# Three hinted widths in the experts' conditional first layer, and side work in smaller, evenly spaced steps

## The chip, the cores and the metric

One core of one Trainium2 chip. The metric is device time in microseconds of one execution. The kernel before takes 965.94 us (median of 3 runs, 965.71 to 967.29).

## The reference

Attention with a window of 128 keys over 4 sequences of 576 tokens, then a mixture of 8 experts with the two best of each token, then a gated feed-forward block:

```
attn = softmax(q k^T / 8 + bias, masked) v           # 2304 tokens x 512
noisy = x w_gate + log1p(exp(x w_noise)) * noise      # 2304 x 8
top2  = the two largest of each row, weights by softmax
for e in range(8):                                    # w1: 512 x 1024, w2: 1024 x 512
    out[rows of e] += weight * (relu(x[rows] @ w1[e]) @ w2[e])
xn  = out / rms(out) * rms_g
y   = (silu(xn @ w_gate2) * (xn @ w_val)) @ w_out     # 512 -> 1536 -> 512
```

How many rows an expert gets is known only when the routing has run. With the inputs of the case, experts 1 to 7 get 571, 575, 544, 545, 556, 606 and 584 rows.

## The kernel before, in words

The program is one hand-ordered stream. After attention and routing, experts 0 to 7 follow one another, then the gated block runs in products over quads of token tiles. Each expert has room for 640 rows (CAP). Every product is made of three float16 products of high and low halves (hi*hi, lo*hi, hi*lo), so each value leaves PSUM twice: ACT writes the high half, DVE the low one.

An expert e of 1 to 7 has five stages on TensorE (PE):

- **first layer**, rows 0 to 383: 8 column blocks of 12 matmuls of 384 columns (`first_steps`, L199). After each block ACT writes hh (L204) and DVE hl (L205). PSUM has three buffers for the even blocks and two for the odd ones.
- **second layer**, three blocks of 128 rows, 24 matmuls of 512 columns each (`second_steps`, L259). Each block ends with an ACT copy ys (L316) and a store to ybuf on SP's queue (L322).
- **tail**: the first layer for rows 384 to 639 (`tail_steps`, L234), 96 matmuls. Its width depends on the row count: the table `WIDTHS` has 160, 192, 224 and 256 columns, and the program holds one copy of the 96 matmuls for each. A register of PE, `arm`, counts how many of the first three widths are too small, and two nested conditions (`by_arm`, L215) pick the copy. The widest copy stands first in the program, the narrowest last; a copy that isn't the last ends with a branch over the rest. Then ACT and DVE take the four pairs of blocks out of PSUM (hh L244, hl L245).
- a **fourth block** of the second layer (again L259), which needs the four hl in turn.
- the **halves** block (`halves_steps`, L275) for rows 512 to 639, whose second half runs in full only where arm is over 1 (L281).

`drive` interleaves side work with these stages. Each side is a generator with a due column and a pace: when the columns that PE has been given pass the due column, the side's next step is emitted, and the due column grows by the pace. An expert is some 112,000 such columns long (first layer to 36,864, second layer to 73,728, tail to 92,160, fourth block to 104,448). The sides are:

- `weight_steps`: 8 loads of 512 KB for expert e+1, in 16 steps of one ACT conversion (L136) and one DVE subtraction (L138), from 2,000 at 3,000. The first three loads are issued at the end of the expert ahead (`ahead`, at 106,000).
- `m2_steps`: six 512 KB pieces of the gated block's float64 weights per expert, from 46,000 at 3,100. A piece takes three steps: (1) load of a later piece, and ACT's conversion hi of the piece before (L767), (2) DVE's lo of the piece before (L770), ACT's square sq (L779) and three DVE operations u (L780 to L782), (3) DVE's r (L785).
- `weight_sums`: sums of weights for the later products, a chunk of six steps on DVE (L817), ACT (L820) and GpSimd (L823). Experts 3, 4, 5 and 6 make one chunk each, from 30,000 at 5,500, and expert 7 makes three at 3,000 (`SUM0`).
- `row_steps`: transposing loads of the token rows xA and xB (L183).

All loads and stores of these stages stand in one queue, SP's, in program order. The weight loads and the m2 loads share four staging buffers `st`.

Of the kernel before, what the change touches and what calls it, by code (L numbers as in the profile page):

```python
# [31 lines left out]
WIDTHS = (160, 192, 224, 256)  # L32
# [3 lines left out]
SOON, SUM0, SUMS = 3, 3000, 4400  # L36
# [8 lines left out]
def attention_moe_swiglu(  # L45
# [52 lines left out]
    arm = consts.tile([P, E], I32, name="arm")  # L98
# [110 lines left out]
    def by_arm(value, ways, lo=0):  # L209

        if len(ways) == 1:
            ways[0]()
            return
        half = len(ways) // 2
        with tc.If(value > lo + half - 1) as cmp:  # L215
            by_arm(value, ways[half:], lo + half)
        with cmp.Else():
            by_arm(value, ways[:half], lo)

    def tail_steps(w1h, w1l, xT, cs, arm):  # L220

        hh = hpool.tile([P, FC, GW], F16, name="hh")
        hl = hpool.tile([P, FC, GW], F16, name="hl")
        yield hh, hl
        w = cs.stop - cs.start
        hps = [ps.tile([P, 2, w], F32, name=f"mm{i % 2}", bufs=MM[i % 2]) for i in range(FC // 2)]

        def columns(most):
            for f in range(FC):
                n = 0  # L230
                for w1, xo in ((w1h, 0), (w1l, 0), (w1h, KC)):
                    for c in range(KC):
                        now = most if n else w
                        nc.tensor.matmul(hps[f // 2][:, f % 2, :now], w1[:, c, f * P:(f + 1) * P],  # L234
                                         xT(xo + c, slice(cs.start, cs.start + now)),
                                         start=(n == 0), stop=(n == 3 * KC - 1))
                        n += 1

        by_arm(arm, [functools.partial(columns, x) for x in WIDTHS])
        mean = 3 * KC * WIDTHS[1]  # L240
        for i, hp in enumerate(hps):
            yield mean
            fs = slice(2 * i, 2 * i + 2)
            nc.scalar.activation(hh[:, fs, :w], hp, AF.Relu)  # L244
            nc.vector.scalar_tensor_tensor(hl[:, fs, :w], hp, 0.0, hh[:, fs, :w], op0=OP.max, op1=OP.subtract)  # L245
            yield mean
# [18 lines left out]
    def halves_steps(yp, hh, hl, w2h, w2l, i, arm):  # L265
# [15 lines left out]
        with tc.If(arm > 1) as cmp:  # L281
            rows(1, 3 * FC)
# [11 lines left out]
    def expert_steps(e, *pieces):  # L294
# [6 lines left out]
        if pieces == (LAST,) and e:  # L301
            steps = tail_steps(w1h, w1l, x, *pieces, arms[e])
# [4 lines left out]
        for cs in pieces:  # L307
            for c in range(cs.start, cs.stop, P):
                yp = ps.tile([P, DM], F32, name="acc", bufs=2)
                halved = e and c + P == CAP  # L310
                if halved:
                    yield from halves_steps(yp, hh, hl, w2h, w2l, (c - pieces[0].start) // P, arms[e])
# [15 lines left out]
    with ExitStack() as actx:  # L328
# [403 lines left out]
        wide = work.tile([P, E], F32, name="wide", bufs=1)  # L732
        nc.vector.tensor_scalar(wide, tot, float(GW + WIDTHS[0]), None, op0=OP.is_gt)
        for i, w in enumerate(WIDTHS[1:-1]):
            nc.vector.scalar_tensor_tensor(arm if i == len(WIDTHS) - 3 else wide, tot, float(GW + w), wide,
                                           op0=OP.is_gt, op1=OP.add)
# [20 lines left out]
    def m2_steps(parts):  # L757

        sts, last = [], None
        for i in range(len(parts) + 3):  # L760
# [3 lines left out]

            if last:
                r, sc, hi, lo = last
                nc.scalar.activation(hi, r, AF.Copy, scale=sc)  # L767
            yield
            if last:
                nc.vector.scalar_tensor_tensor(lo, r, sc, hi, op0=OP.mult, op1=OP.subtract)  # L770
            if not 2 <= i < len(parts) + 2:
                continue
            _, sc, hi, lo = parts[i - 2]

            wl, wh = (sts[i - 2].rearrange("p (n two) -> p n two", two=2)[:, :, j] for j in range(2))
            sq = dec.tile([P, DM], F32, name="sq")
            u = dec.tile([P, DM], I32, name="u")
            r = dec.tile([P, DM], F32, name="r")
            nc.scalar.activation(sq, wh.bitcast(F32), AF.Square)  # L779
            nc.vector.tensor_scalar(u, wh, 3, 0x3FFFFFFF, op0=OP.logical_shift_left, op1=OP.bitwise_and)  # L780
            nc.vector.scalar_tensor_tensor(u, wl, 29, u, op0=OP.logical_shift_right, op1=OP.bitwise_or)  # L781
            nc.vector.scalar_tensor_tensor(u, wh, -0x40000000, u, op0=OP.bitwise_and, op1=OP.bitwise_or)  # L782
            yield

            nc.vector.scalar_tensor_tensor(r, sq, 1.265625 * 2.0 ** -30, u.bitcast(F32), op0=OP.is_ge, op1=OP.mult)  # L785
# [64 lines left out]
    EARLIER = {3: [(0, 0)], 4: [(1, 0)], 5: [(0, 1)], 6: [(1, 1)]}  # L850
    BESIDE = len(EARLIER)
# [3 lines left out]

    def read_arms():
        _, values = nc.values_load_multi_w_load_instructions(arm[0:1, 0:E], engines=[EngineType.PE])
        arms.update(enumerate(values))
        yield

    def ahead(e):
        if e < E:
# [6 lines left out]
          (40000, 4000, mix()), (60000, 4000, read_arms()), (70000, 5000, ahead(2)))  # L869
    for e in range(1, E - 1):  # L870
        drive(itertools.chain(*(expert_steps(e, cs) for cs in HALVES)),
              (2000, 3000, coming.pop(e + 1)), (106000, 5000, ahead(e + 2)),
              (1000, 2000, row_steps(e, HALVES[1])), (46000, 2000, row_steps(e + 1, HALVES[0])),
              (30000, 5500, weight_sums([spool], sw, EARLIER.get(e, ()))),
              (46000, 3100, m2_steps([m2_part(i) for i in range(6 * (e - 1), 6 * e)])))
# [308 lines left out]
    with ExitStack() as c:  # L1184
        mp, xpool = block_pools(c, "tile")
        xq = xpool.tile([P, 28, QW], F16, name="xq")
        for at in chunks[BESIDE:BESIDE + SOON]:
            sw[at] = [xpool.tile([P, 2, 2, 2, P], F16, name=f"sw{at[0]}{at[1]}_{j}") for j in range(2)]
        drive(itertools.chain(*(expert_steps(E - 1, cs) for cs in HALVES)), (1000, 2000, row_steps(E - 1, HALVES[1])),
              (0, SUM0, weight_sums([spool, mp], sw, chunks[BESIDE:BESIDE + SOON])),  # L1190
# [100 lines left out]
```

## Time and profile before

The profiled execution took 972.34 us by the same clock as the runs, and its span from the first to the last instruction is 970.6 us.

| | |
|---|---|
| median of 3 runs | 965.94 us |
| profiled execution: time, span | 972.34 us, 970.6 us |
| PE busy | 930.8 us (96%) |
| DVE busy | 647.5 us (67%) |
| ACT busy | 453.9 us (47%) |
| GpSimd busy | 214.5 us (22%) |
| mean granted TensorE clock | 0.991 |

Busy time is the union of an engine's instructions. A matmul's end is modelled, so consecutive matmuls overlap in the record, and a gap shorter than this overlap isn't shown as idle. [...] "issue" is idle time in which an engine waited for nothing that the profile shows. PE's sequencer, which reads the instructions and runs ahead of the matrix unit, has rows of its own, named PEldq.

### The profile page before, as it was taken

Reading aid. Unit: us, or ns where it says so; the run is one execution under the profiler, and the core shown is the slowest. Engines: PE = TensorE matmul, PEld = TensorE weight load, DVE = VectorE, ACT = ScalarE, POOL = GpSimd, SP = SyncE. Lnnn points to the kernel's source line nnn. Section 1 sums busy time; section 2 is a strip of 40 time slices with the busy share of each in tenths; the row PEclk is TensorE's granted clock in tenths of the full one; section 3 lists DMA queues with packets and bytes.
Section 4 is the critical chain, followed back from the end, with each engine's and each line's share of the span. In section 5 each row is a group of like instructions: output and inputs, shape, how many; then the busy total and the mean of one; then the engine's idle time right before and its main releaser. Section 6 shows DMA issues by size and latency. Waiting matters only on the chain.

```text
span 970.6 us, 19059 instructions
## 1 busy us (share of the span) xinstructions
PE 930.8 (96%) x7478; PEld 661.0 (68%) x7478; DVE 647.5 (67%) x1482; ACT 453.9 (47%) x911; POOL 214.5 (22%) x255
## 2 busy tenths in 40 slices
PE   7998999999989989999999899999999999999997
PEld 5997888656656555556565586687488558848864
DVE  6799975536677878777777267798169618925840
ACT  7997873444354544454634245335224413532320
POOL 5566763000000101010103235610501131030000
PEclk9999999999999999999999999999999999999999
DMA  7988674767584849393931332510511250032000
GB/s 222 314 238 235 188 183 151 196 189 219 145 270 126 265 130 276 103 271 112 270 118 37 96 87 46 130 34 1 138 37 33 42 133 22 12 76 46 1 13 35
DMA packets 146691, 127.19 MB, mean 131 GB/s; under 512 B 98320, under 2 KB 117264, under 8 KB 146576
## 3 DMA queue, kind: packets, MB, share of 16 engines
q1 hardware_dynamic: 140816, 106.73, 40.5%
q0 software_dynamic: 5760, 18.88, 6.1%
q8 instruction: 78, 1.28, 0.6%
q14 instruction: 37, 0.30, 0.1%
HBM read 76.55 MB, written 26.74 MB: 106 GB/s over the span
## 4 chain that ended last, share of the span: by engine, by line
PE 61%; DVE 19%; DMA 6%; ACT 4%; issue 4%; SPq 2%; POOL 2%; another core or an unknown queue 0%; DVEq 0%; POOLq 0%; ACTq 0%
PE mm L1113 22%; PE acc L1085 11%; PE mm L199 7%; PE acc L259 7%; PE acc L454 4%; DMA st<-in_moe_w 3%; DVE w2l L138 2%; PE mm L440 2%; DVE sums L817 2%; PE mm L234 2%; PE mm L412 2%; PE acc L275 2%; DVE u L781 2%; DVE hl L205 1%; DVE u L782 1%
## 5 line engine op out<-in xcount | busy, mean ns | idle before, releaser
L259 PE MATMUL acc<-w2h,hh 128*128 128x512 f16 x264 | 101.7, 385 | 7.2 <-issue 4.7
L259 PE MATMUL acc<-w2h,hl 128*128 128x512 f16 x264 | 101.9, 386 | 4.3 <-DVE hl L245 3.5
L259 PE MATMUL acc<-w2l,hh 128*128 128x512 f16 x264 | 101.5, 385 | 0.0
L823 POOL TENSOR_TENSOR sw<-sums,sw 128x256 f16<-128x256 f32 x28 | 26.2, 945 | 335.7 <-ACT sw L820 335.6
L259 PEld LDWEIGHTS <-hh 128*128 128x128 f16 x528 | 51.7, 99 | 68.2 <-issue 8.1
L199 PE MATMUL mm<-xA,w1h 128*128 128x384 f16 (+2 forms) x576 | 97.3, 308 | 0.8 <-issue 0.8
L1085 PE MATMUL acc<-oh__3309,pgh 128*128 128x512 f16 (+2 forms) x228 | 83.3, 368 | 0.1
L1085 PE MATMUL acc<-ol__3310,pgh 128*128 128x512 f16 (+2 forms) x228 | 83.3, 368 | 0.0
L1085 PE MATMUL acc<-oh__3309,pgl 128*128 128x512 f16 (+2 forms) x228 | 83.2, 368 | 0.0
L199 PEld LDWEIGHTS <-w1h 128*128 128x128 f16 x640 | 59.7, 98 | 33.7 <-issue 2.3
L1113 PE MATMUL mm<-xq,sw 128*128 128x256 f16 x672 | 78.1, 273 | 3.0 <-DMA xq<-xg 3.0
L205 DVE SCALAR_TENSOR_TENSOR hl<-mm,hh 128x384 f16<-128x384 f32 (+2 forms) x80 | 39.7, 500 | 60.3 <-ACT hh L204 60.3
L1085 PEld LDWEIGHTS <-pgh 128*128 128x128 f16 x456 | 44.1, 98 | 49.2 <-ACT pgh L1065 0.6
L1113 PEld LDWEIGHTS <-sw 128*128 128x128 f16 x672 | 65.6, 98 | 11.5 <-issue 3.5
L454 PE MATMUL acc<-v,pf 128*128 128x96 f32 x544 | 72.1, 275 | 0.0
L432 ACT ACTIVATE pr<-ss,nm 128x256 f32<-128x256 f32 (+1 forms) x144 | 63.1, 488 | 10.4 <-DVE nm L423 8.6
L454 PEld LDWEIGHTS acc<-v,pf 128*128 128x128 f32 x544 | 67.9, 195 | 0.1
L423 DVE CUSTOM_DVE_ANT_0 ss<-mm,bias 128x256 f32<-128x256 f32 (+1 forms) x144 | 54.0, 397 | 13.7 <-PE mm L412 6.6
L1122 DVE TENSOR_TENSOR gt<-mm,p 128x512 f32<-128x512 f32 x24 | 16.6, 691 | 66.1 <-PE mm L1113 62.6
L1134 ACT ACTIVATE p<-mm 128x256 f32<-128x256 f32 x48 | 18.3, 382 | 77.5 <-PE mm L1113 75.5
L199 PE MATMUL mm<-xA,w1l 128*128 128x384 f16 (+2 forms) x288 | 53.8, 308 | 0.0
L259 PEld LDWEIGHTS <-hl 128*128 128x128 f16 x264 | 26.1, 99 | 40.6 <-DVE hl L245 7.7
(215 smaller groups left out, 2076.5 us busy)
## 6 DMA issues: line engine op xcount, KB each, us to landing
st<-in_moe_w SPq DMA_DIRECT2D x64, 512.0 KB, 4.4
raw<-in_qkv SPq DMA_DIRECT2D x17, 512.0 KB, 5.5
ybuf<-ys SPq DMA_DIRECT2D x33, 256.0 KB, 2.5
st<-in_moe_w_gate SPq DMA_DIRECT2D x12, 512.0 KB
st<-in_moe_w_val SPq DMA_DIRECT2D x12, 512.0 KB, 4.3
st<-in_moe_w_out SPq DMA_DIRECT2D x12, 512.0 KB, 4.4
v<-in_qkv SPq DMA_DIRECT2D x18, 279.0 KB, 7.3
out<-ys SPq DMA_DIRECT2D x17, 256.0 KB, 2.0
```

The lines of the kernel that those rows point to most:

```text
L138: nc.vector.scalar_tensor_tensor(*last, op0=OP.mult, op1=OP.subtract)
L199: nc.tensor.matmul(hp[:, :w], w1[:, c, f * P:(f + 1) * P], xT(xo + c, cs), start=(n == 0), stop=(n == 3 * KC - 1))
L205: nc.vector.scalar_tensor_tensor(hl[:, f, hs], hp[:, :w], 0.0, hh[:, f, hs], op0=OP.max, op1=OP.subtract)
L234: nc.tensor.matmul(hps[f // 2][:, f % 2, :now], w1[:, c, f * P:(f + 1) * P], xT(xo + c, slice(cs.start, cs.start + now)), start=(n == 0), ...
L259: nc.tensor.matmul(yp, hx[:, f, i * P:(i + 1) * P], w2[:, f, :], start=(n == 0), stop=(n == 3 * FC - 1))
L275: nc.tensor.matmul(yp[d * P // 2:(d + 1) * P // 2, j * DM // 2:(j + 1) * DM // 2], hx[:, f, at:at + P // 2], w2[:, f, d * DM // 2:(d + 1) ...
L423: nc.vector.tensor_tensor_reduce(out=d["ss"][:, j, c0:], in0=d["sp"][:, j, c0:], in1=bias[kind][:, heads(d["hp"])[j], c0:], scale=-1.0 / K ...
L432: nc.scalar.activation(d["pr"][:, j, c0:], d["ss"][:, j, c0:], AF.Exp, scale=-1.0, bias=d["nm"][:, j:j + 1])
L454: nc.tensor.matmul(xps[t, hp // 2][:, h % 4, :VN], ph[:, j, kk, :], v32[t - 1 + kk][:, h * DV:h * DV + VN], start=(kk == k0), stop=(kk == 1))
L823: nc.gpsimd.tensor_tensor(out=here[k][1], in0=x, in1=here[k][0], op=OP.subtract)
L1085: nc.tensor.matmul(op[:, ds], px[:, f, cs], w[:, f, ds], start=(k == 0), stop=(k == 3 * GC - 1))
L1113: nc.tensor.matmul(pp, w(a, pa, c), xq[:, 4 * b + 2 * pb + c, :], start=(n == 0), stop=(n == 5))
```

## The change

Four things are edited.

1. `WIDTHS` loses 160. Two flags per expert (more than 192 rows in the tail, more than 224) replace the count in `arm`. The tail has three copies. The outer condition takes the narrow copy, last in the program, in its Else part; the halves condition reads the first flag.
2. The flags are no longer read all at once during expert 0. `read_arms(e)` reads two of them ahead of the third second-layer block of expert e, and puts a branch hint there, whose value is the first flag.
3. `m2_steps` is cut differently: ACT's hi and sq and two of the u operations in step one, the third u and the lo of the piece before in step two, r in step three. It starts at 30,000 and runs at 3,800.
4. The weight steps run at 2,500 in place of 3,000. Experts 4 and 6 make one chunk of sums each, from 41,000 at 8,000, and expert 7 makes five at 2,500.

```
-WIDTHS = (160, 192, 224, 256)
+WIDTHS = (192, 224, 256)
-SOON, SUM0, SUMS = 3, 3000, 4400
+SOON, SUM0, SUMS = 3, 2500, 4400
-    arm = consts.tile([P, E], I32, name="arm")
+    arm = consts.tile([P, E, 2], I32, name="arm")
...
+    def read_arms(e):
+        _, arms[e] = nc.values_load_multi_w_load_instructions(arm[0:1, e], engines=[EngineType.PE])
+        tc.mark_branch_hint_location(f"tail{e}", hint=arms[e][0], engines=[EngineType.PE])
+
+    def by_arm(e, ways):
+
+        wide, full = arms[e]
+        with tc.If(wide, label=f"tail{e}") as cmp:
+            with tc.If(full) as cmp2:
+                ways[2]()
+            with cmp2.Else():
+                ways[1]()
+        with cmp.Else():
             ways[0]()
...
-        mean = 3 * KC * WIDTHS[1]
+        mean = 3 * KC * WIDTHS[0]
...
-        with tc.If(arm > 1) as cmp:
+        with tc.If(arms[e][0]) as cmp:
...
+                if e and c + P == GW:
+                    read_arms(e)
...
+            here = 2 <= i < len(parts) + 2
             if last:
                 r, sc, hi, lo = last
                 nc.scalar.activation(hi, r, AF.Copy, scale=sc)
-            yield
+            if here:
+                wl, wh = (sts[i - 2].rearrange("p (n two) -> p n two", two=2)[:, :, j] for j in range(2))
+                sq = dec.tile([P, DM], F32, name="sq")
+                u = dec.tile([P, DM], I32, name="u")
+                nc.scalar.activation(sq, wh.bitcast(F32), AF.Square)
+                nc.vector.tensor_scalar(u, wh, 3, 0x3FFFFFFF, op0=OP.logical_shift_left, op1=OP.bitwise_and)
+                nc.vector.scalar_tensor_tensor(u, wl, 29, u, op0=OP.logical_shift_right, op1=OP.bitwise_or)
+            yield
+            if here:
+                nc.vector.scalar_tensor_tensor(u, wh, -0x40000000, u, op0=OP.bitwise_and, op1=OP.bitwise_or)
             if last:
                 nc.vector.scalar_tensor_tensor(lo, r, sc, hi, op0=OP.mult, op1=OP.subtract)
...
-    EARLIER = {3: [(0, 0)], 4: [(1, 0)], 5: [(0, 1)], 6: [(1, 1)]}
-    BESIDE = len(EARLIER)
+    EARLIER = {4: [(0, 0)], 6: [(1, 0)]}
+    BESIDE = 4
...
-          (40000, 4000, mix()), (60000, 4000, read_arms()), (70000, 5000, ahead(2)))
+          (40000, 4000, mix()), (70000, 5000, ahead(2)))
...
-              (2000, 3000, coming.pop(e + 1)), (106000, 5000, ahead(e + 2)),
+              (2000, 2500, coming.pop(e + 1)), (106000, 5000, ahead(e + 2)),
...
-              (30000, 5500, weight_sums([spool], sw, EARLIER.get(e, ()))),
-              (46000, 3100, m2_steps([m2_part(i) for i in range(6 * (e - 1), 6 * e)])))
+              (41000, 8000, weight_sums([spool], sw, EARLIER.get(e, ()))),
+              (30000, 3800, m2_steps([m2_part(i) for i in range(6 * (e - 1), 6 * e)])))
...
-              (0, SUM0, weight_sums([spool, mp], sw, chunks[BESIDE:BESIDE + SOON])),
+              (0, SUM0, weight_sums([spool, mp], sw, [(0, 1), (1, 1), *chunks[BESIDE:BESIDE + SOON]])),
```

Three places show how the order moves. The first is PE ahead of expert 1's tail. Before (line numbers of the kernel before):

```order
L259 LDWEIGHTS hl
L259 MATMUL acc<-w2h,hl 128x512
L215 COMPARE_AND_BRANCH x2
L234 LDWEIGHTS w1h
L234 MATMUL mm_4007<-xB,w1h 128x256
```

And in the change (its own line numbers; L263 is the second layer, L238 the tail):

```order
L263 MATMUL acc<-w2h,hl 128x512
L210 TENSOR_LOAD arm
L1287 BRANCH_PREFETCH_HINT
L263 LDWEIGHTS hh
L263 MATMUL acc<-w2h,hh 128x512
...
L263 MATMUL acc<-w2h,hl 128x512
L216 COMPARE_AND_BRANCH
L217 COMPARE_AND_BRANCH
L238 LDWEIGHTS w1h
L238 MATMUL mm_4011<-xB,w1h 128x256
```

The read and the hint stand 48 PE instructions (24 matmuls of 512 columns) ahead of the first branch, and two copies of 192 instructions lie between that branch and the narrow copy.

The second is DVE around the tail of expert 3 (hl is the low half taken out of PSUM; u, r and the low half vl are the m2 step). Before:

```order
L782 SCALAR_TENSOR_TENSOR u<-st,u 128x512
L245 SCALAR_TENSOR_TENSOR hl<-mm_5764,hh 128x2x256
L785 SCALAR_TENSOR_TENSOR r<-sq,u 128x512
L245 SCALAR_TENSOR_TENSOR hl<-mm_5765,hh 128x2x256
L770 SCALAR_TENSOR_TENSOR vl__3308<-r,gain,vh__3307 128x512
L780 TENSOR_SCALAR u<-st 128x512
L781 SCALAR_TENSOR_TENSOR u<-st,u 128x512
L782 SCALAR_TENSOR_TENSOR u<-st,u 128x512
L245 SCALAR_TENSOR_TENSOR hl<-mm_5766,hh 128x2x256
L785 SCALAR_TENSOR_TENSOR r<-sq,u 128x512
L245 SCALAR_TENSOR_TENSOR hl<-mm_5767,hh 128x2x256
```

In the change (L249 is hl, L777, L778 and L781 are u, L783 is lo, L790 is r):

```order
L249 SCALAR_TENSOR_TENSOR hl<-mm_5569,hh 128x2x256
L790 SCALAR_TENSOR_TENSOR r<-sq,u 128x512
L249 SCALAR_TENSOR_TENSOR hl<-mm_5570,hh 128x2x256
L777 TENSOR_SCALAR u<-st 128x512
L778 SCALAR_TENSOR_TENSOR u<-st,u 128x512
L249 SCALAR_TENSOR_TENSOR hl<-mm_5571,hh 128x2x256
L781 SCALAR_TENSOR_TENSOR u<-st,u 128x512
L783 SCALAR_TENSOR_TENSOR vl__3306<-r,gain,vh__3305 128x512
L249 SCALAR_TENSOR_TENSOR hl<-mm_5572,hh 128x2x256
```

Between two hl there are now at most two m2 operations, where there were up to four, and lo no longer stands right behind the r on which it depends through ACT.

The third is SP's queue from the end of expert 1 into expert 2. Before:

```order
L322 DMA ybuf<-ys 128x512
L116 DMA st<-in_moe_w 128x4x256 x2
L320 DMA ybuf<-ys 64x2x256 x2
L116 DMA st<-in_moe_w 128x4x256
L183 DMA_TRANSPOSE xB<-xrows 128x8x128 x2
L116 DMA st<-in_moe_w 128x4x256
L116 DMA st<-in_moe_w 128x2x512 x4
L183 DMA_TRANSPOSE xA<-xrows 128x8x128
L763 DMA st<-in_moe_w_gate 128x1024
```

In the change (L326 is the store of the halves block, L766 the m2 load):

```order
L326 DMA ybuf<-ys 64x2x256 x2
L116 DMA st<-in_moe_w 128x4x256
L183 DMA_TRANSPOSE xB<-xrows 128x8x128
L116 DMA st<-in_moe_w 128x4x256
L183 DMA_TRANSPOSE xB<-xrows 128x8x128
L116 DMA st<-in_moe_w 128x2x512 x4
L766 DMA st<-in_moe_w_gate 128x1024 x3
L183 DMA_TRANSPOSE xA<-xrows 128x8x128 x2
```

The fourth weight load has moved ahead of the second xB transpose, and three m2 loads ahead of the xA transposes.

## Rows read from the trace of the kernel before

**Rows 1.** PE's waits, 200 to 640 us: us in total, times, longest.

```profile
PE acc L259 <- issue: 4.7, 2, 2.6
PE mm L234 <- issue: 4.4, 4, 2.2
PE acc L259 <- DVE hl L245: 3.5, 3, 1.6
PE acc L259 <- ACT hh L244: 2.5, 4, 0.8
```

**Rows 2.** Windows: experts 1 to 7, cut at each one's first matmul.

```profile
core 0: us, PE busy (x) PEld busy (x) DVE busy (x) ACT busy (x) POOL busy (x), PEclk, DMA share, GB/s
204.58:252.01 47.43, 47.43 (x340) 29.32 (x338) 31.93 (x53) 23.51 (x44) 0.00 (x0) 1.00 0.61 173
252.01:302.21 50.20, 47.77 (x340) 29.16 (x339) 35.00 (x59) 24.31 (x47) 0.00 (x0) 1.00 0.67 200
302.21:353.09 50.88, 47.28 (x340) 27.71 (x339) 39.06 (x66) 24.64 (x49) 4.29 (x4) 1.00 0.69 198
353.09:405.88 52.79, 49.81 (x340) 29.53 (x339) 40.79 (x69) 26.64 (x52) 4.29 (x4) 0.97 0.64 191
405.88:456.18 50.30, 48.10 (x341) 29.08 (x339) 38.15 (x64) 23.81 (x48) 4.29 (x4) 1.00 0.72 200
456.18:511.18 55.00, 52.95 (x386) 33.41 (x385) 43.04 (x73) 26.40 (x52) 4.30 (x4) 0.97 0.63 188
511.18:566.47 55.29, 52.65 (x387) 33.34 (x385) 26.01 (x58) 17.72 (x38) 14.88 (x18) 0.97 0.29 73
```

**Rows 3.** Windows inside experts 4, 6 and 7 with a lowered clock; columns as above.

```profile
400.30:403.60 3.30, 3.30 (x18) 1.40 (x18) 3.13 (x6) 0.12 (x1) 0.00 (x0) 0.50 0.00 0
499.30:502.60 3.30, 3.30 (x9) 1.22 (x8) 2.12 (x5) 1.67 (x3) 0.00 (x0) 0.50 0.02 5
553.90:557.20 3.30, 2.76 (x7) 1.04 (x8) 1.73 (x4) 2.38 (x4) 0.00 (x0) 0.50 0.35 107
```

**Rows 4.** Line L215 near the tails of experts 1, 2 and 6: ns min/median/max.

```profile
L215 PEldq COMPARE_BRANCH  x2: 82/1886/3690, 231.9 to 235.6; - x2
L215 PEldq COMPARE_BRANCH  x2: 82/3011/5940, 279.7 to 285.8; - x2
L215 PEldq COMPARE_BRANCH  x3: 70/208/3867, 483.5 to 494.9; - x3
```

**Rows 5.** Line L857, the read of all eight arms in expert 0.

```profile
L857 PEldq TENSOR_LOAD <-arm x1: 777/777/777, 190.3 to 190.3; - x1
```

**Rows 6.** Timeline of PE: first tail and next second-layer matmul, experts 1 and 3.

```profile
235.75 0.53 PE L234 MATMUL mm<-xB,w1h 128*128 128x256 f16 x4
...
243.88 0.38 PE L259 MATMUL acc<-w2h,hh 128*128 128x512 f16 x1
...
334.34 0.49 PE L234 MATMUL mm<-xB,w1h 128*128 128x256 f16 x4 [0.81 <-issue]
...
341.31 0.38 PE L259 MATMUL acc<-w2h,hh 128*128 128x512 f16 x1
```

**Rows 7.** Timeline of DVE, ACT and PE, third and fourth pair of expert 3's tail.

```profile
343.52 0.74 DVE L770 SCALAR_TENSOR_TENSOR vl__3308<-r,gain,vh__3307 128x512 f16<-128x512 f32 x1
344.18 0.42 DVE L780 TENSOR_SCALAR u<-st 128x512 int32<-128x512 int32 x1
...
345.97 0.68 DVE L245 SCALAR_TENSOR_TENSOR hl<-mm,hh 128x512 f16<-128x512 f32 x1
346.57 0.68 DVE L785 SCALAR_TENSOR_TENSOR r<-sq,u 128x512 f32<-128x512 f32 x1
...
347.28 0.72 ACT L767 ACTIVATE vh__3307<-r,gain 128x512 f16<-128x512 f32 x1 [3.36 <-DVE r L785]
...
346.71 0.39 PE L259 MATMUL acc<-w2h,hl 128*128 128x512 f16 x1 [1.58 <-DVE hl L245]
```

**Rows 8.** ACT's waits, 200 to 560 us: us in total, times, longest.

```profile
ACT w1h L136 <- DMA st<-in_moe_w: 28.3, 15, 4.0
```

More of the change, by code (lines that the diff above doesn't have):

```diff
@@ L207, in first_steps, with tail_steps @@
             yield 6 * w
-    def by_arm(value, ways, lo=0):
-        if len(ways) == 1:
-            ways[0]()
[L213 to L220, printed above, removed]
+    def read_arms(e):
[9 more added lines that the diff above has]
+        with cmp.Else():
+            ways[0]()
+    def tail_steps(w1h, w1l, xT, cs, e):
         hh = hpool.tile([P, FC, GW], F16, name="hh")
@@ L237, in columns @@
                         n += 1
-        by_arm(arm, [functools.partial(columns, x) for x in WIDTHS])
-        mean = 3 * KC * WIDTHS[1]
+        by_arm(e, [functools.partial(columns, x) for x in WIDTHS])
+        mean = 3 * KC * WIDTHS[0]
         for i, hp in enumerate(hps):
@@ L263, in second_steps, with halves_steps @@
                 yield 6 * DM
-    def halves_steps(yp, hh, hl, w2h, w2l, i, arm):
+    def halves_steps(yp, hh, hl, w2h, w2l, i, e):
         def rows(j, most):
@@ L301, in expert_steps @@
         if pieces == (LAST,) and e:
-            steps = tail_steps(w1h, w1l, x, *pieces, arms[e])
+            steps = tail_steps(w1h, w1l, x, *pieces, e)
         else:
@@ L310, in expert_steps @@
                 halved = e and c + P == CAP
+                if e and c + P == GW:
+                    read_arms(e)
                 if halved:
-                    yield from halves_steps(yp, hh, hl, w2h, w2l, (c - pieces[0].start) // P, arms[e])
+                    yield from halves_steps(yp, hh, hl, w2h, w2l, (c - pieces[0].start) // P, e)
                 else:
@@ L731, in attention_moe_swiglu @@
         nc.vector.scalar_tensor_tensor(over, most, float(CAP), few[:, :1], op0=OP.is_gt, op1=OP.max)
[L732 to L736, printed above, removed]
+        for i, w in enumerate(WIDTHS[:-1]):
+            nc.vector.tensor_scalar(arm[:, :, i], tot, float(GW + w), None, op0=OP.is_gt)
     m2w = ctx.enter_context(tc.tile_pool(name="m2w", bufs=1, side="right", reuse_waits="tile"))
@@ L767, in m2_steps @@
                 nc.scalar.activation(hi, r, AF.Copy, scale=sc)
+            if here:
[5 more added lines that the diff above has]
+                nc.vector.scalar_tensor_tensor(u, wl, 29, u, op0=OP.logical_shift_right, op1=OP.bitwise_or)
             yield
+            if here:
+                nc.vector.scalar_tensor_tensor(u, wh, -0x40000000, u, op0=OP.bitwise_and, op1=OP.bitwise_or)
             if last:
                 nc.vector.scalar_tensor_tensor(lo, r, sc, hi, op0=OP.mult, op1=OP.subtract)
-            if not 2 <= i < len(parts) + 2:
+            if not here:
                 continue
+            yield
             _, sc, hi, lo = parts[i - 2]
-            wl, wh = (sts[i - 2].rearrange("p (n two) -> p n two", two=2)[:, :, j] for j in range(2))
-            sq = dec.tile([P, DM], F32, name="sq")
-            u = dec.tile([P, DM], I32, name="u")
             r = dec.tile([P, DM], F32, name="r")
[L779 to L782, printed above, removed]
-            yield
             nc.vector.scalar_tensor_tensor(r, sq, 1.265625 * 2.0 ** -30, u.bitcast(F32), op0=OP.is_ge, op1=OP.mult)
```

4 lines of the change are left out of this document (removed).

## The prediction

> **What bounds the kernel now.** I read PE's waits first. PE is busy for 96% of the span, so the kernel is bound by TensorE, and only its idle time and its clock can give anything back. In the stretch of the experts [rows 1] the waits are of two kinds. 9.1 us (4.7 and 4.4) are "issue", at the first matmul behind a branch: PE waited for no engine and no load. 6.0 us (3.5 and 2.5) are the fourth block of the second layer waiting for hl and hh of the tail, which DVE and ACT write.
>
> Then I cut the trace at the first matmul of each expert [rows 2]. Expert 1 takes 47.43 us and is busy throughout: that is the price of an expert at a tail of 192 columns. The others are measured against it.
>
> - Experts 2, 4 and 5 have the same work and take 50.20, 52.79 and 50.30 us: 2.8, 5.4 and 2.9 us too many.
> - Expert 3 has the tail of 160 columns. Its tail takes 341.31 - 334.34 = 6.97 us, where expert 1's takes 243.88 - 235.75 = 8.13 us [rows 6]: 1.16 us less. So it should take 46.27 and takes 50.88 us: 4.6 too many.
> - Experts 6 and 7 have a tail of 224 columns and the full halves block. 88 matmuls by 32 columns more at 2.4 GHz are 1.2 us, and 23 further steps of 256 columns are 2.5 us, so they should take 51.1 us. They take 55.00 and 55.29 us: 3.9 and 4.2 too many.
>
> The sum is **23.8 us** too many, where the idle rows show 15.1. The rest hides in "busy" time: PE busy is 47.77 to 49.81 us in experts 2 to 5. A part of it is the clock. It stood at 0.50, the 1.2 GHz level, for at least 3.3 us in experts 4, 6 and 7 [rows 3], each time around or behind one of the long waits, and at 1.00 elsewhere in these experts. 3.3 us at half speed cost up to 1.7 us each, 5 us in all. The rest is waits shorter than the modelled overlap of matmuls. So a stall costs more than its idle row, and what takes the stalls away takes this too.
>
> **The change, part by part.**
>
> *The branches.* In expert 1 the first branch took 3.69 us on PE's sequencer, but PE went on without a gap. In expert 2 it took 5.94 us, and the stall was 2.2 us, the longest of its kind. So the sequencer runs some 3.7 us ahead while 512-column matmuls drain, and what a branch takes beyond that is a stall [rows 1, 4]. At the exit of expert 6, behind a copy with shorter matmuls, the cover is less: 3.87 us of branch left some 2 us of stall [rows 1, 4]. The same expert's other two branches took 0.07 and 0.21 us, though the second of them jumped over a copy of 192 instructions. The long ones all jumped over two copies, or went on from a jump over two. I read this as the jump reaching code that isn't on the chip yet.
>
> After the change experts 1 to 5 jump over two copies to the narrow one, with the hint 24 matmuls of 512 columns, about 5.2 us, ahead of the branch. With the cover of 3.7 us that is 8.9 us against at most 5.94. They then fall through without an exit branch. Experts 6 and 7 jump over one copy, and at the exit over one copy in place of two, so I take 0.2 us for each, hidden. All 9.1 us of "issue" should go.
>
> [...]
>
> *The reads of the flags.* One read of eight registers took 0.78 us on the sequencer [rows 5]. Seven reads of two take no more than that each, and the hint is bounded by the shortest branch, 0.08 [rows 4], and that read. Behind the 3.7 us cover they cost nothing; without it, at most 7 x 1.6 = 11 us. I take nothing, since PE shows no wait at the read of before.
>
> *The narrow width.* Only expert 3 changes, from 160 to 192 columns: **+1.2 us** [rows 6].
>
> *The m2 steps.* In expert 3's tail ACT's conversion of an m2 piece stands ahead of hh and waited 3.36 us for DVE's r. DVE's lo and three u (0.74, 0.42 and twice about 0.7 us, together 2.5) stand ahead of the third hl, which came so late that PE waited 1.58 us [rows 7]. After the change two m2 operations at most stand between two hl, 1.4 us (0.7 and 0.74), and r is at least one pair ahead of the conversion that needs it. In the tail's 8.1 us DVE has four hl of 0.6, one r, one pair of u and two pairs of third u and lo: 2.4 + 0.7 + 1.1 + 2.9 = 7.1 us. Each pair has until the fourth block reaches it, some 3 us after the last pair is computed. So the 6.0 us should go.
>
> *The paces.* An m2 piece costs DVE 3.2 us (0.42, four of about 0.7). It comes every 11,400 columns, or 4.75 us, in place of 9,300, or 3.9 us: 68% of DVE where it was 83%. In return the weight steps (0.68 us, like r) come every 1.04 us in place of 1.25, and with an hl of some 0.5 us (384 columns against the tail's 512 at 0.68) every 1.9 us, which is 12 x 384 columns at 2.4 GHz, that is about 91% in the first layer where it was about 81%. Over an expert DVE's work fits: 43.04 us at most in a row of 51.1 [rows 2], and experts 3 and 5 lose a chunk of 4.3 us. Expert 7 gains two chunks, 8.6 us on its 26.01 in 51.1. What DVE does late is next in line: the hl of the first layer's last blocks, and the ACT conversions there, which already waited 28.3 us for weight loads [rows 8], up to 4.0 us at a time. PE hardly felt those, since it has five PSUM buffers, some 6 us of lead. The loads should come sooner: the ys ahead of the first three in SP's queue no longer wait behind a late m2 conversion, and the fourth load has one transpose fewer ahead of it. I leave 0.5 us of new stall for each of experts 2 to 6, **+2.5 us**; the ends are 0 and 1.0 each.
>
> *Behind the experts.* The first gated tiles follow expert 7 by a chain of gathers, DVE, ACT and a transpose. That chain moves up with the tail's hh, but not quite as much as PE, which ends 4.2 us sooner: **+0.7 us**, between 0 and 2.
>
> **The sum.** 23.8 - 1.2 - 2.5 - 0.7 = 19.4 us less. The profiled execution took 972.34 us (span 970.6), 6.4 us more than the median of 965.94, and some of the stalls may be longer under the profiler. I take 1 us off for that: **18.4 us less, 947.5 us** against the median. With no new stall at all it is 23.8 - 1.2 = 22.6 less, 943.3. With both new terms at their upper ends (5 and 2) and two dips of the clock left (3.4), it is 12.2 less, 953.7.
>
> **The rivals.**
>
> - *The hint fetches nothing.* [...] Then experts 1 to 5 keep a jump over two copies. Before, their stalls at the tail's start cost between 0 (expert 1) and 2.8 us (expert 2), and 4.4 us of idle over five experts; with one dip of the clock that is 4.4 + 1.7 = 6.1 of the gain lost: 953.6.
> - *The tails still wait.* DVE is at 91% in the first layer, and m2 begins there; if it enters the tail some 3 us late, the fourth block goes on waiting. The 6.0 us of idle and expert 4's dip (1.7) stay: 947.5 + 7.7 = 955.2.
> - *Slower: ACT stuck behind weight loads.* ACT's order is fixed, and at 2,500 more weight steps stand ahead of the later hh of the first layer. If the loads come no sooner than now (waits up to 4.0 us [rows 8]) and the earlier steps add the wait for one more load, an hh is later than the 6 us of lead, and PE stands still in six experts for about 4 us each, with a dip of 1.7: 6 x 5.7 = 34 us against the 18.4 gained, 982. The point from which it decides is an hh of blocks 4 to 6 more than 6 us behind its matmuls. Against it: the loads should be sooner.
> - *Nothing comes of it*: a third of this last loss would do.
>
> **How the numbers follow.** The forecast has 0.62, the idle hint 0.13, the waiting tails 0.14, the slower case 0.07 and the even one 0.04. The range reaches from the forecast without new stalls, 943.3, past the two middle cases to 957, where both of their losses stand in part; 0.11 lies above it by the cases and a little below. 0.2% is 1.9 us, about what a measurement can tell from no change. Faster by more than that takes the first three cases, 0.89; the same 0.04; slower 0.07.
>
> **What would show it.** In the profile after, experts 1 to 5 should take 47.4 to 48.4 us each and 6 and 7 about 51.1 to 52, with the clock at 1.00 in all. The "issue" waits at the tail and behind it should be gone, with the first branch under 1 us in experts 1 to 5 and the exits under 0.5 in 6 and 7; a first branch of 3 to 6 us would show an idle hint. The waits for the tail's hl and hh should be under 1 us in sum. I would be wrong if waits for the first layer's hh or hl (L204, L205) of over 1 us per expert came in their place, or if the first gated matmuls waited over 2 us for their transposes.

## The result, and the profile after

The changed kernel took **952.7 us** (median of 4 runs, 950.77 to 953.92) and the kernel before, beside it, 966.62 (965.71 to 967.47): ratio **0.9848**, 95% interval 0.9829 to 0.9868. That is 13.9 us less, where 18.4 were forecast; the time lies in the range given. The same kernel was measured twice more, on two chips: 0.9803 (0.9785 to 0.9821), 946.73 against 965.13, and 0.9834 (0.9803 to 0.9866), 954.02 against 970.41. So the gain differed from set to set, by the medians 13.9, 18.4 and 16.4 us; what differs in the traces is told below, its cause stays open.

The profiled execution took 953.77 us. First the page's span and its line for PE:

```profile
span 952.0 us, 19116 instructions
PE 926.3 (97%) x7478; PEld 663.3 (70%) x7478; DVE 647.7 (68%) x1481; ACT 457.7 (48%) x911; POOL 210.2 (22%) x255
```

The experts, cut as in [rows 2], and as the eighth row a window of half clock behind them. Columns: the window and its length, busy us (instructions) of PE, PEld, DVE, ACT and POOL, the granted clock, the DMA share and GB/s.

```profile
204.35:251.75 47.40, 47.40 (x339) 29.39 (x337) 35.45 (x58) 25.11 (x45) 0.00 (x0) 1.00 0.68 181
251.75:300.48 48.73, 47.58 (x341) 29.41 (x339) 35.53 (x58) 24.89 (x45) 0.00 (x0) 1.00 0.77 206
300.48:347.88 47.40, 47.40 (x340) 29.40 (x338) 35.25 (x58) 24.54 (x45) 0.00 (x0) 1.00 0.84 211
347.88:395.29 47.41, 47.41 (x340) 29.41 (x339) 39.59 (x66) 26.18 (x49) 3.31 (x4) 1.00 0.75 212
395.29:442.75 47.46, 47.46 (x341) 29.38 (x339) 34.71 (x58) 24.02 (x45) 0.00 (x0) 1.00 0.83 211
442.75:493.84 51.09, 51.09 (x387) 33.09 (x385) 40.13 (x68) 25.57 (x49) 3.44 (x4) 1.00 0.71 196
493.84:547.14 53.30, 51.21 (x386) 33.10 (x385) 34.75 (x72) 22.56 (x48) 21.43 (x26) 1.00 0.30 71
547.91:551.33 3.42, 3.42 (x36) 3.42 (x34) 0.00 (x0) 0.38 (x1) 0.00 (x0) 0.50 0.38 85
```

Five of the seven now take their own work and nothing else: 47.4 us at a tail of 192 columns, 51.09 at 224. Expert 2 has 1.3 us too many and expert 7 2.2. The clock is at full speed in all seven; the dips of experts 4, 6 and 7 [rows 3] are gone, and one of 3.4 us stands behind the last.

PE's waits in the same stretch (us in total, times, longest), which answer to [rows 1]:

```profile
PE mm L1051 <- DMA xq<-xg: 2.1, 1, 2.1
PE mm L1051 <- DVE vt L1063: 1.4, 2, 1.3
PE mm L238 <- issue: 1.2, 1, 1.2
```

The waits for hl and hh of the tail are gone, 6.0 us. Of the 9.1 us of "issue", 1.2 are left, in expert 2, but not at the tail's start: PE stands still in the middle of the narrow copy, after 49 of its 96 matmuls, and goes on 5.8 us after the branch had ended. New is the first row, the first gated matmul waiting for its transpose. The second was there before (1.3).

PE as it goes on in expert 2's tail:

```profile
288.39 0.41 PE L238 MATMUL mm<-xB,w1h 128*128 128x192 f16 x3 [1.15 <-issue]
```

The first branch of experts 1 and 2 (ns min/median/max), which took 3.69 and 5.94 us [rows 4]:

```profile
L216 PEldq COMPARE_BRANCH  x1: 735/735/735, 231.6 to 231.6; - x1
L216 PEldq COMPARE_BRANCH  x1: 3565/3565/3565, 279.0 to 279.0; - x1
```

### The profile page after: what moved, and what is told of

Same layout as the page of the kernel before. It is cut to its first block, busy times and chain, and to the rows that moved or that the text cites. A ratio compares the mean times of both kernels' runs of the same rounds, so it can differ in the third digit from the quotient of the medians.

```text
span 952.0 us, 19116 instructions
## 1 busy us (share of the span) xinstructions
PE 926.3 (97%) x7478; PEld 663.3 (70%) x7478; DVE 647.7 (68%) x1481; ACT 457.7 (48%) x911; POOL 210.2 (22%) x255
## 4 chain that ended last, share of the span: by engine, by line
PE 84%; DVE 7%; DMA 3%; ACT 2%; issue 2%; SPq 1%; POOL 1%; another core or an unknown queue 0%; DVEq 0%; ACTq 0%; POOLq 0%
PE mm L1113 23%; PE acc L263 17%; PE mm L199 14%; PE acc L1085 11%; PE mm L238 6%; PE acc L460 4%; PE mm L446 3%; PE acc L279 2%; PE mm L418 2%; DMA xq<-xg 2%; DVE ss L429 1%; DVE sums L822 1%; SPq L1014 1%; DVE w2l L138 1%; DVE pgl L1067 1%
## 5 line engine op out<-in xcount | busy, mean ns | idle before, releaser
L263 PE MATMUL acc<-w2h,hl 128*128 128x512 f16 x264 | 100.1, 379 | 0.0
L263 PE MATMUL acc<-w2l,hh 128*128 128x512 f16 x264 | 100.1, 379 | 0.0
L263 PE MATMUL acc<-w2h,hh 128*128 128x512 f16 x264 | 100.1, 379 | 0.0
L828 POOL TENSOR_TENSOR sw<-sums,sw 128x256 f16<-128x256 f32 x28 | 22.4, 811 | 331.1 <-ACT sw L825 330.3
L263 PEld LDWEIGHTS <-hh 128*128 128x128 f16 x528 | 51.6, 98 | 59.4 <-issue 0.2
L1122 DVE TENSOR_TENSOR vt<-mm,vt 128x512 f32<-128x512 f32 (+1 forms) x72 | 43.3, 602 | 13.3 <-PE mm L1113 9.7
```

The lines of the kernel that those rows point to most:

```text
L263: nc.tensor.matmul(yp, hx[:, f, i * P:(i + 1) * P], w2[:, f, :], start=(n == 0), stop=(n == 3 * FC - 1))
L828: nc.gpsimd.tensor_tensor(out=here[k][1], in0=x, in1=here[k][0], op=OP.subtract)
L1122: nc.vector.tensor_tensor(out=o, in0=x, in1=y, op=OP.add)
```

## The experiments

Each set below ran on one chip, with the kernel before beside it. The kernel before took 970.68 us in the first set (e1 to e4), 965.13 in the second (e5 to e8) and 970.41 in the third (e9 to e12). Ratios are to it. This table has the length of each expert in us, from its first matmul to the next one's (expert 7: to the first gated matmul), out of one profiled execution each, cut as above. An expert without stalls takes 47.4 (46.27 at 160 columns, expert 3 with four widths, by the prediction's estimate), 51.1 for 6 and 7.

| kernel | 1 | 2 | 3 | 4 | 5 | 6 | 7 | sum |
|---|---|---|---|---|---|---|---|---|
| before [rows 2] | 47.43 | 50.20 | 50.88 | 52.79 | 50.30 | 55.00 | 55.29 | 361.89 |
| e5, before again | 47.56 | 49.13 | 50.69 | 51.17 | 51.10 | 53.06 | 55.32 | 358.03 |
| after | 47.40 | 48.73 | 47.40 | 47.41 | 47.46 | 51.09 | 53.30 | 342.79 |
| e6, after again | 47.40 | 47.41 | 47.41 | 47.41 | 47.56 | 51.09 | 51.10 | 339.38 |
| e9, after again | 47.40 | 47.41 | 47.41 | 47.41 | 47.41 | 51.09 | 53.56 | 341.69 |
| e1, branches alone | 47.40 | 47.41 | 51.75 | 52.06 | 50.38 | 52.13 | 53.20 | 354.33 |
| e2, side work alone | 49.83 | 51.23 | 50.16 | 48.63 | 51.25 | 53.03 | 53.79 | 357.92 |
| e3, no hint | 51.61 | 47.41 | 49.37 | 47.41 | 49.10 | 51.09 | 53.62 | 349.61 |
| e10, no hint | 48.49 | 47.41 | 49.31 | 47.41 | 49.02 | 51.09 | 53.52 | 346.25 |
| e11, m2 alone | 47.40 | 51.26 | 51.65 | 48.70 | 52.25 | 52.47 | 53.09 | 356.82 |
| e12, paces alone | 47.40 | 47.41 | 47.41 | 47.41 | 47.45 | 51.09 | 53.51 | 341.68 |

**e1, e2: the two halves of the change, each alone.** e1 is the kernel before with this (and the rest of the branches, flags and hint):

```diff
-WIDTHS = (160, 192, 224, 256)
+WIDTHS = (192, 224, 256)
...
+                if e and c + P == GW:
+                    read_arms(e)
```

> The kernel before with the three widths, the flags and the hint of the change, and its side work as before. Theory (branches and tails are separate losses that add): the issue waits of 9.1 us at the tails go but for about 1.2, expert 3 pays 1.2, the waits of the fourth block for hl and hh of the tail stay near 6 us, and the time is 6 to 8 us below before, 958 to 960. Rival (one hides the other): with the branches gone PE reaches the fourth block earlier, so the waits for hl and hh grow to 9 us or more, and the time is within 4 us of before, 962 or more.

e2 is the changed kernel with these lines, and the branches that go with them, as before:

```diff
-WIDTHS = (192, 224, 256)
+WIDTHS = (160, 192, 224, 256)
```

> The changed kernel with the four widths and the branches of before. Theory (they add): the waits for hl and hh of the tail fall below 1 us, the issue waits stay near 9 us, and the time is 5 to 8 us below before, 958 to 961. Rival: the branch stalls had let the side work catch up or the reverse, and the time is within 3 us of before, 963 or more; or the side work alone holds nearly all of the gain, 955 or less.

e1: 967.43 us, 0.9975 (0.9955 to 0.9995). e2: 964.88 us, 0.9929 (0.9903 to 0.9955). By the medians they gain 3.3 and 5.8 us, 9.1 together, where the whole change gains 13.9 to 18.4 (it was not run in this set). PE's waits, 200 to 640 us, of e1 and then of e2:

```profile
PE acc L263 <- DVE hl L249: 4.7, 3, 1.6
PE acc L263 <- ACT hh L248: 2.9, 4, 0.8
```

```profile
PE mm L234 <- DMA ybuf<-ys: 6.1, 3, 2.1
PE acc L259 <- issue: 4.0, 2, 2.3
PE mm L234 <- issue: 3.3, 2, 2.3
```

In e1 the branch stalls are gone, and the tails wait 7.6 us in place of 6.0. In e2 the tails don't wait, and PE stands 13.4 us behind branches in place of 9.1, with three dips of the clock (0.97 in experts 2, 3 and 5). So the rival of e1 holds by its time (within 4 us of before), though its waits grew to 7.6 and not to 9; e2's 5.8 us lie within its theory's 5 to 8, its issue waits not near its 9. Neither half gets its price alone. That each loss hid a part of the other is argued; in e2 the branches themselves also took longer, the first one of expert 1 6.09 us where it was 3.69. (The releaser in e2's first row, the store of ys, is only the last semaphore event before the start. These waits are the branch's: e3 shows it.)

The table shows more of the tails. In e1 the m2 steps are in every expert as before, but experts 1 and 2, which make no sums of weights, take 47.40 and 47.41 us. Experts 3, 4 and 5, which make a chunk each, take 3.0 to 4.7 us more, and every wait of e1 for hl and hh of the tail stands in experts 3 to 6. So the bundle of m2 operations alone makes no tail wait; the chunk beside it does, as far as experts of one kernel can be compared. No run takes the chunk out alone.

**e3, e10: the hint taken out of the changed kernel**, on two chips; e9 is the changed kernel beside e10.

```diff
-        tc.mark_branch_hint_location(f"tail{e}", hint=arms[e][0], engines=[EngineType.PE])
```

> The changed kernel without the line that marks the hint. Theory (the hint brings the narrow copy in): the first branches of experts 1, 3 and 4, 0.45 to 0.87 us with the hint, go back to 3 to 6 us, PE's issue waits at the tails rise from 1.2 to 3 us or more, and the time is 2 to 6 us above the changed kernel's 952.7, 955 to 959. Rival (the hint fetches nothing, the narrow copy last in the row pays by itself): first branches and time as with the hint, 951 to 954.

> The changed kernel, for the comparison of the three others of this call on one chip. The ratio was 0.9848 at first and 0.9803 the second time; expected 0.980 to 0.986.

> The changed kernel without the hint, beside the changed kernel on the same chip. Theory: first branches of 5 to 6.5 us in experts 1, 3 and 5, as in the first run without the hint, and 4 to 8 us above the changed kernel of this call. Rival (on a chip whose branches are shorter the 3.7 us by which the sequencer runs ahead cover them): first branches of 3 to 4 us and within 2 us of the changed kernel.

e3: 958.67 us, 0.9872 (0.9843 to 0.9902). e10: 958.41 us, 0.9891 (0.9851 to 0.9931), 4.4 us above e9's 954.02. First branches of experts 1, 3 and 5 in e3, and PE around the first of them:

```profile
L215 PEldq COMPARE_BRANCH  x1: 6347/6347/6347, 234.0 to 234.0; - x1
...
L215 PEldq COMPARE_BRANCH  x1: 5760/5760/5760, 333.0 to 333.0; - x1
...
L215 PEldq COMPARE_BRANCH  x1: 5480/5480/5480, 429.8 to 429.8; - x1
```

```profile
237.63 0.38 PE L262 MATMUL acc<-w2h,hl 128*128 128x512 f16 x1
240.38 0.53 PE L237 MATMUL mm<-xB,w1h 128*128 128x256 f16 x4 [2.38 <-DMA ybuf<-ys]
```

The branch began at 234.0, took 6.35 us, and PE went on at 240.38, as it ended: 2.4 us of stall. Without the hint experts 1, 3 and 5 cost 1.1 to 4.2 us more; with it nothing. Experts 2 and 4 show no stall in e3 and e10 either (for 4 the theory had one): their branches, over the same distance in the code, took 1.44 and 0.87 us in e3.

The DMA rows show the fetch itself. They have a queue for instructions, q8, with packets of 16 KB (on the changed kernel's page 73 of them, 1.20 MB; columns: packets, MB, share of 16 DMA engines). Of expert 1, first the changed kernel from the hint to the branch (227.3 to 231.6 us), then e3 during the branch (234.0 to 240.35):

```profile
q8 instruction: 1, 0.02, 1.4%
```

```profile
q8 instruction: 1, 0.02, 1.1%
```

In e3's 4.3 us ahead of that branch q8 has no packet. It is the same in experts 3 and 5 of e3 and in 1, 3 and 5 of e10: none in the stretch ahead, one during the branch. In experts 2 and 4 a packet comes ahead of the branch even without a hint. With the hint, the packet stands between hint and branch in experts 1 to 5 of e6 and e9. In the changed kernel's first profile it comes only during the branch in experts 2 and 5, whose branches took 3.57 and 2.89 us. So the hint fetches, and is worth some 4 us (4.4 by e10 and e9).

**e4: the first two combined tiles taken together**, against the wait behind expert 7.

```diff
-        sqs = [mp.tile([P, 1], F32, name=f"sq{i}", bufs=1) for i in range(FIRST)]
...
+        sq = mp.tile([P, FIRST], F32, name="sq0", bufs=1)
+        x3s = []
+        for i in range(FIRST):
+            x3s.append(mixed(i, *ys[i]))
+            if not i:
+                square(mp, x3s[0], sq[:, :1])
+        yield
+        square(mp, x3s[1], sq[:, 1:])
...
```

> The changed kernel with the first two combined tiles taken together: both mixed ahead of the tail's last hl in expert 7, the first squared ahead of the last hh, and one root and one refinement for both. The second tile's transpose is issued at about 543.7 us in place of 545.34. Theory (the new wait behind expert 7 is this chain): the 2.1 us wait of the first gated matmul falls below 0.8, the half-speed stretch of 3.4 us behind it goes or shrinks, and the time is 2 to 4 us below the changed kernel's 952.7, 949 to 951. Rival: the chain is held by the gathers (the second tile's rows land at 536.8) and hl of the last pair now comes late, so the wait moves into the fourth block and the time is 952 to 954.

954.38 us, 0.9826 (0.9798 to 0.9855); the wait is still 2.1 us. Its first transposes and the gated matmul:

```profile
543.26 3.50 SPq L913 DMA_TRANSPOSE xq<-xg  x2
...
547.86 0.38 PE L1049 MATMUL mm<-xq,gh 128*128 128x128 f16 x4 [2.14 <-DMA xq<-xg]
```

The second transpose now goes out right behind the first, as meant. Neither theory nor rival holds: the fourth block doesn't wait, and PE waits for the first tile's, 4.6 us from issue to use, and that was issued at 543.26, no earlier than in the changed kernel (542.57, below). The run moved the second tile's chain, and PE waits for the first tile. That the wait hangs on this chain is argued from the rows further below.

**e5, e6: both kernels once more.**

> The kernel before, once more, for a second profile of it. Theory (the long branches and the clock's dips are no accident of one execution): by the stage starts experts 1 to 7 again take 18 us or more too many, with first branches of 3 us or more in at least three of the experts 1, 2, 3 and 5, and the exits of 6 and 7 near 4 us. Rival (the profiled execution of 972.34 us was an unlucky one and the 6 us above the median were stalls): span of 966 or less, and not over 18 us too many. The time is that of the kernel before, ratio 1.000 within 0.003.

> The changed kernel, once more, on a chip where the kernel before and the others of this call run too. Theory: the ratio is again 0.983 to 0.987; in its experts at most 5 us too many, with a wait of about 2 us and a half-speed stretch behind expert 7. Rival (the gain differs from chip to chip): a ratio outside 0.980 to 0.990.

e5: 964.89 us, 0.9996 (0.9981 to 1.0012), span 964.1. The theory's stalls and branches hold, of its dips one is there (in expert 7); the rival holds in the span alone. The first branches of experts 1, 2 and 5 took 3.8, 5.4 and 5.3 us, the second of 3 4.3, the exits of 6 and 7 3.6 and 4.2. By the table it has 358.03 - 338.05 = 20.0 us too many (five tails of 47.4, with expert 3 at 46.27, and two of 51.1), so the stalls are there in both profiled executions; but it is 3.9 less than in the first, whose span was 6.5 longer. The clock stays at 1.00 in its experts 1 to 6. e6: 946.73 us, 18.4 less. Its experts have hardly a stall left; expert 7 takes 51.10, as its work alone does, and the gated matmuls wait for a transpose once, 0.9 us, for the second tile. The ratio lies between the theory's 0.983 and the rival's 0.980, so neither holds.

**e7: the hint one block earlier.**

```diff
-                if e and c + P == GW:
+                if e and c == P:
```

> The changed kernel with the read of the flags and the hint one block earlier, 48 matmuls of 512 columns (10.4 us) ahead of the branch in place of 24 (5.2). Theory (the hint starts a fetch that takes some 4 to 6 us and must be done by the branch): the first branches of experts 2 and 5, 3.57 and 2.89 us with the late hint, fall below 1, the 1.2 us issue wait in expert 2 goes, and the time is 0 to 2 us below the changed kernel's. Rival (what the hint brought is replaced before it is used): first branches of 4 to 6 us in experts 1, 3 and 5 as without a hint, and the time 3 to 6 us above it.

947.31 us, 0.9813 (0.9794 to 0.9832), e6 beside it 0.9803 (0.9785 to 0.9821): no difference. The first branches of experts 1 to 5 took 0.37, 1.51, 0.34, 0.45 and 0.34 us, in e6 1.07, 1.59, 1.21, 0.46 and 1.45, and none is seen by PE. The rival falls: what the hint brought is still there 48 matmuls later. Whether it spares expert 2 its 1.2 us elsewhere is open; in e9 that stall didn't come at all.

**e8: the gathers held back**, through a GpSimd subtraction that reads the last hl, and their chain started 18,000 columns later.

```diff
+        nc.gpsimd.tensor_tensor(out=gone, in0=tails[0][:, FC - 1, :P], in1=tails[0][:, FC - 2, :P], op=OP.subtract)
         ys = [gather(mp, i) for i in range(FIRST)]
...
-              (3 * GW * (FC * KC + FC * KC) + 2000, 3100, combine_first(mp, xq[:, :2 * KC])))
+              (3 * GW * (FC * KC + FC * KC) + 20000, 3100, combine_first(mp, xq[:, :2 * KC])))
```

> The changed kernel, with the six gathers behind expert 7's third block held back until the hl of the tail's last pair is written, by a small GpSimd subtraction that reads it. Theory (the gathers that run then make the last hh of the tail late: its matmuls end at 534.5 us in the trace, its ACT instruction starts at 537.3): without gathers beside it that hh starts within 0.6 us of the end of its matmuls, as the other three pairs do. The gathers then start some 6 us later and the first gated matmul waits for its transposes 6 to 9 us, so the time is 4 to 8 us above the changed kernel's. Rival (something else holds that hh): it starts 2 us or more behind its matmuls again.

955.68 us in one run, 9.0 above e6 where the theory had 4 to 8. The last hh was prompt and the gated matmul waited 7.9 us, as the theory has it. But in e6, on the same chip, the last hh was as prompt with the gathers beside it. So this run tells nothing of them.

**e11, e12: the side work cut in two.** e11 has the m2 steps of the change and the weight steps and sums of before; e12 the paces and sums of the change and the m2 operations bundled as before.

```diff
-              (2000, 2500, coming.pop(e + 1)), (106000, 5000, ahead(e + 2)),
+              (2000, 3000, coming.pop(e + 1)), (106000, 5000, ahead(e + 2)),
...
-              (41000, 8000, weight_sums([spool], sw, EARLIER.get(e, ()))),
+              (30000, 5500, weight_sums([spool], sw, EARLIER.get(e, ()))),
```

> The changed kernel with its branches and the m2 pieces in three even steps at 3,800 columns from 30,000, but the weight steps, the weight sums and their places as before. Theory (the tail waited for m2 operations ahead of its hh and hl): PE's waits for hh and hl of the tail are under 1 us in sum in experts 2 to 6 but for the extra sums of experts 3 and 5, and the time is within 2 us of the changed kernel of this call. Rival (the load on DVE as a whole delays the tail, so that the sums in experts 3 and 5 count): waits of 2 to 6 us in experts 3 and 5, and 3 to 8 us above it.

```diff
-            if here:
-                wl, wh = (sts[i - 2].rearrange("p (n two) -> p n two", two=2)[:, :, j] for j in range(2))
...
+            wl, wh = (sts[i - 2].rearrange("p (n two) -> p n two", two=2)[:, :, j] for j in range(2))
```

> The changed kernel with all its paces, but the operations of an m2 piece bundled as before (square and three u in one step, then r, then conversion and lo). Theory (the bundle of three u and an early conversion stand ahead of hh and hl): waits of 1 to 4 us for hh and hl of the tail in experts 2 to 6, and 1 to 6 us above the changed kernel of this call. Rival (the longer stretch with less in it is what counts): no waits over 0.5 us there, and within 1 us of it.

e11: 966.61 us, 0.9944 (0.992 to 0.9969), 12.6 above e9. e12: 953.41 us, 0.982 (0.979 to 0.9851), the same as e9. Both theories fall, and e12 is as its rival has it; e11 loses more than its rival said, and at another place. PE's waits of e11, its first branch in expert 2, and then all that PE waited for in e12 between 200 and 560 us:

```profile
PE acc L263 <- ACT ys L322: 7.9, 4, 3.0
PE mm L238 <- issue: 3.2, 2, 1.9
...
L216 PEldq COMPARE_BRANCH  x1: 5895/5895/5895, 280.1 to 280.1; - x1
```

```profile
PE mm L1049 <- DMA xq<-xg: 2.1, 1, 2.1
```

With three even m2 steps alone PE waits for ACT's ys in the second layer, which none of the other kernels shows, and expert 2 meets a branch of 5.9 us in spite of the hint (q8's packet comes during the branch). The four waits for ys stand one each in experts 3 to 6, the four that make a chunk of sums. With the paces alone, three u bundled again, nothing is late, though in experts 1 to 6 of e12 lo and three u stand together ahead of a tail's last hl. Which of the paces and sums does it (weight steps at 2,500, the two chunks moved from experts 3 and 5 to 7, or the later, slower sums) was not tried apart.

## Why the prediction was right, and where it was not

*The stalls too many: the mis-sized term.* The sum went from 23.8 us and took 1 us off for an execution that was 6.4 us above the median. e5 has 20.0 in a span of 964.1: the discount should have been about 4. Then the parts come to 20.0 - 1.2 for expert 3, 18.8 at most. e6 measured 18.4 on its chip with no stall left. That this is the forecast's own figure is partly luck: the discount was 2.8 us too small, and the 2.5 for the paces and the 0.7 behind the experts, 3.2 together, didn't come there. The first result has 3.6 us of stalls left up to the gated matmuls (1.3 in expert 2, 2.2 behind expert 7), and 18.8 - 3.6 = 15.2, less up to 1.7 for the dip behind them, lies inside its interval (13.9; by the ratio's ends 12.8 to 16.5).

*The branches* went as forecast, but for the remainder in expert 2. Without the hint the first branches of experts 1, 3 and 5 take 4.9 to 6.3 us (e3, e10), with it 0.5 to 2.9 in the changed kernel's three profiles, and 0.5 to 3.6 in experts 2 and 4. The rival that the hint fetches nothing, 0.13 by the author's estimate, fell. The long branches were read as jumps over two copies to code that isn't on the chip yet. In the kernel before a packet of q8 lies within each of the six branches over 3 us (3.69, 5.94, 4.31, 4.87, 3.87 and 4.46 us in experts 1, 2, 3, 5, 6 and 7); but the distance alone doesn't decide, since expert 4's first branch jumped over two copies as well and took 0.32 us in the kernel before. What was read as a cover of 3.7 us measures 4.0: in all six long branches of e3 and e10 the branch less its stall is 3.97 (6.35 less 2.38, 5.76 less 1.79). The 1.2 us left in expert 2 are no part of this: the branch of 3.57 us was covered, and PE stopped later, within the copy. It stopped behind the same 49th matmul in e4 (0.3 us) and e11 (1.3), and each time a packet of q8 ended 1.2 to 1.4 us before it went on. That this is the copy's next piece is likely, not shown. The exits of experts 6 and 7, 3.9 and 4.5 us before, take 0.28. The reads of the flags, put at nothing, take 0.54 to 0.72 us each on the sequencer and show no wait of PE.

*The tails* stopped waiting, as forecast, **for another reason than the one given**. The step on the m2 operations argued that the bundle of three u and the early conversion stand ahead of hl and hh. e12 keeps the bundle and doesn't wait, and in e1 experts 1 and 2 have bundle and conversion as before and don't wait either. The waits stood where a chunk of sums came on top. What pays is the package of paces and places, less of it at a time and the sums elsewhere; its parts were not tried apart. The prediction had put the paces down as a cost of 2.5 us. They cost nothing: PE has no wait for hh or hl left in any expert. The slower rival, ACT stuck behind weight loads, fell too. ACT's wait for them, 28.3 us in [rows 8], is now, over the same stretch:

```profile
ACT w1h L136 <- DMA st<-in_moe_w: 20.6, 16, 3.3
```

*One sum for both parts* was right only because both were changed: the prediction priced branches and tails as if each could be had alone, and e1 and e2 show that they can't.

*Its own signs.* One sign of being wrong came: the first gated matmul waited 2.1 us, and the bound was 2. Experts 2 and 7 and the first branches of 2 and 5 lie outside what was to be seen; the clock, the exits and the tails' waits lie inside, and no wait for the first layer's hh or hl came. Two slips stand in the working and don't touch the forecast: for the even case a third of 34 us is said to be enough, where 18.4 is over half, and PE's busy time in experts 2 to 5 is 47.28 to 49.81 us in [rows 2], not from 47.77. The 2.4 and 1.2 GHz of the working stand for columns per ns: no row gives a clock in GHz, but in the trace of before 30 matmuls of 512 columns start 0.216 us apart at a granted clock of 1.00 (225.14 to 231.40 us), 2.37 columns per ns, and three 0.425 us apart at 0.50 (401.04 to 401.89), 1.2. At 2.37 the wider tail and the longer halves of experts 6 and 7 are again 1.2 and 2.5 us.

*Behind the experts* 0.7 us was taken, between 0 and 2. It was 2.1 and a dip of 3.4 us at half speed, up to 1.7 more, in the first result, 2.2 without a dip in e9, and nothing for the first tile in e6. The two traces show where it begins. In the changed kernel first (the last tail matmuls, the last hh, the first transpose, the first gated matmul), then the same in e6:

```profile
533.91 0.55 PE L238 MATMUL mm<-xB,w1h 128*128 128x224 f16 x4
...
537.28 0.60 ACT L248 ACTIVATE hh<-mm 128x512 f16<-128x512 f32 x1 [4.48 <-remote]
...
542.57 1.25 SPq L913 DMA_TRANSPOSE xq<-xg  x1
...
547.14 0.39 PE L1051 MATMUL mm<-xq,gh 128*128 128x128 f16 x4 [2.09 <-DMA xq<-xg]
```

```profile
530.69 0.55 PE L238 MATMUL mm<-xB,w1h 128*128 128x224 f16 x4
...
531.27 0.60 ACT L248 ACTIVATE hh<-mm 128x512 f16<-128x512 f32 x1 [1.73 <-PE mm L238]
...
536.95 1.26 SPq L913 DMA_TRANSPOSE xq<-xg  x1
...
541.71 0.40 PE L1051 MATMUL mm<-xq,gh 128*128 128x128 f16 x4
```

In e6 hh starts as its matmuls end (531.24), in the other 2.8 us after (534.46). The square of the first tile stands behind hh in ACT's order, so the chain to the transpose is later too, by 2.4 us against the end of the tail's matmuls, and the matmul that follows 4.6 us behind the transpose waits. A square ahead of that hh, with the rest of the first tile's chain kept as it is, would be the cure to try; it wasn't tried. No run beat the changed kernel beyond its uncertainty.

## What to carry to other kernels

Profile the kernel twice before summing its stalls, and set the stalls against the span of the same execution: here two executions of one kernel differed by 6.5 us, and 3.9 of these were the very stalls that the change removes. Two kinds of stall in one loop need not add up, so price them together, and test each alone before believing in either. Compare the rounds of the loop with each other first: here the rounds without the sums had the same m2 bundle and no late tail. Where an engine is late at one place, look first at how much work comes due in that stretch, and only then at the order of the pieces.

## What the runs showed of the hardware

A long branch was hidden up to a constant: 3.97 us in six first branches of tails, behind matmuls of 512 columns (e3, e10), and 1.82 us in six exits behind the 224-column copy (3.87 less 2.05 and 4.46 less 2.64 in the kernel before, the same in e2 and e5). In the changed kernel's three profiles the instructions' packet goes out 1.7 to 3.5 us after the branch hint in 13 of 15 cases (experts 1 to 5). In the other two it goes out 4.8 and 5.7 us after it, and the branch takes 2.89 and 3.57 us in spite of the hint; in e11's expert 2 it is 8.3 us and 5.9.

The instruction that waits for PE's last tail matmul started late in some sets and not in another, with the same program. In ten profiles (the two kernels' first ones and those of the first and third sets), while gathers were running, the last hh of expert 7 shows its idle time as ended by "remote", 3.8 to 4.6 us long (0.96 in e4, where the square stands ahead of it), and it starts 2.8 to 3.0 us after the tail's matmuls end. In the four of the second set (one of them e8, with its gathers held back) it is not there: in e5 the idle time is 1.73 us and ended by PE, as for the other pairs. That chip also had the lower times for both kernels. What holds the signal back is open.
